# Scaled residual add on one core: the 8-row first piece of x is merged into its 64-row load, and fx is loaded first

## The chip, the core and the metric

The kernel runs on one core of a Trainium2 chip. The metric is the device time of one execution in microseconds (us); lower is better. A core has a matrix engine (PE), a vector engine (DVE), a scalar engine (ACT), a general one (POOL) and a synchronization engine (SP); each runs its own list of instructions, and they wait for one another by semaphores. Data moves between the large memory (HBM) and the on-chip memory (SBUF, 128 partitions) by 16 DMA engines. A transfer is issued by one of the instruction engines, here always SP, and is cut into descriptors, one for each contiguous run of bytes in one partition. A transfer over 128 partitions gives eight descriptors to each of the 16 DMA engines. A packet in the profile is such a descriptor, or the small write that reports a completion.

## The reference

```python
B, S, D = 512, 32, 640
x, fx: bfloat16 (B, S, D);  alpha: bfloat16 (1)

def reference(x, fx, alpha):
    return x + alpha * fx
```

Each tensor has 10,485,760 elements, 20.97 MB. Two are read and one is written: 62.92 MB. Per element there is one multiplication and one addition.

## The kernel before

Each tensor is seen as 128 partitions of 160 rows of 512 elements. One row of one partition is 1 KiB, so a partition holds 160 KiB of a tensor, and a step over rows `a` to `b` moves `b - a` KiB for each partition, in one contiguous run. The text below calls a transfer by that run: 64 rows are 64 KiB runs and 8 MiB in all, 32 rows are 32 KiB runs and 4 MiB, 8 rows are 8 KiB runs and 1 MiB.

A single buffer `buf` of 207 rows for each partition holds everything. Two tables, `F` and `X`, say where the pieces of fx and of x lie in it. The product alpha * fx is written over fx, the sum over x, and later pieces are loaded into places that earlier ones no longer need. Those reuses are what makes some loads wait for additions.

The order of the work is written out in a list, `PLAN`, which is gone through once from top to bottom. There is no loop over tiles on the chip. A line has a letter and the range of rows:

- `f`, `x`: load rows of fx or x (line 86, `nc.sync.dma_start` in `transfer`). All are issued by SP, in this order, into one queue.
- `a`: load alpha into one element (line 112), then spread it over 128 partitions with a 1 x 1 matmul against a row of ones (line 116), and copy the result to `a_f` (line 118).
- `m`: multiply rows of fx by alpha in place on DVE (line 102).
- `t`: add rows of the product to x in place on DVE (line 108).
- `s`: store rows of the sum (line 86).

The plan begins like this, with the steps that the change and the prediction speak of:

```python
PLAN = """
x 0 8
f 0 64
a
x 8 64
f 64 128
m 0 64
t 32 64
x 96 128
t 0 32
x 64 96
```

It goes on with the second multiplication (`m 64 128`), the load `f 128 160` once rows 111 to 128 are added, the load `x 128 160`, the third multiplication, and the remaining additions. The three stores `s 0 64`, `s 64 128` and `s 128 160` come last; the first of them is held back until the addition `t 64 75` is done. The first five loads wait for nothing. `x 96 128` is put where rows of the first piece of fx lay, so SP holds it until `t 32 64` has run; `x 64 96` waits likewise for `t 0 32`. Each multiplication waits for its fx and for `a_f`, and `t 32 64` waits for the product and for the x that it adds to.

SP's instructions run in order: when one waits, those behind it wait too. Once issued, a transfer's descriptors lie in the rings of the DMA engines, which take them one after another; they do not wait for the transfer before to be complete on all engines.

Of the kernel before, what the change touches and what calls it, by code (L numbers as in the profile page):

```python
# [1 line left out]

# [4 lines left out]

ACT = mybir.ActivationFunctionType
ALU = mybir.AluOpType
F32 = mybir.dt.float32  # L10
BF16 = mybir.dt.bfloat16

K = 512
P = 128


F = [(0, 64, 128), (64, 128, 64), (128, 160, 111)]
X = [(0, 64, 0), (64, 128, 143), (128, 160, 79)]
N = 160
ALL = 207  # L20

PLAN = """
x 0 8
f 0 64
a
x 8 64
f 64 128
m 0 64
t 32 64
# [3 lines that stand above are left out]
m 64 128  # L33
t 111 128
f 128 160
t 96 111
t 79 96
x 128 160
m 128 160
t 64 75  # L40
t 75 79
s 0 64
t 128 160
s 64 128
s 128 160
"""
LATE = {"s 0 64": "t 64 75"}


@with_exitstack  # L50
def kernel(
    ctx: ExitStack,
    tc: tile.TileContext,
    x: bass.AP,
    fx: bass.AP,
    alpha: bass.AP,
    out: bass.AP,
):
    nc = tc.nc

    def rows(t, a, b):

        v = t.flatten_outer_dims().rearrange("(p n) d -> p (n d)", p=P)
        assert v.shape[1] == N * K
        return v[:, a * K : b * K]

    consts = ctx.enter_context(tc.tile_pool(name="consts", bufs=1))
    psum = ctx.enter_context(tc.tile_pool(name="psum", bufs=1, space=bass.MemoryType.PSUM))
    whole = ctx.enter_context(tc.tile_pool(name="whole", bufs=1))
    ctx.enter_context(tc.manual_schedule())  # L70

    sync = mybir.DependencyInfo(mybir.DependencyClass.Sync, mybir.DependencyReason.DATA)
    buf = whole.tile([P, ALL * K], x.dtype, name="buf")
    done = []
    said = {}
    lanes = {}

    def at(pieces, a, b):

        s, _, h = next(p for p in pieces if p[0] <= a < p[1])  # L80
        e, _, g = next(p for p in pieces if p[0] < b <= p[1])
        assert h - s == g - e
        return buf[:, (a + h - s) * K : (b + h - s) * K]

    def transfer(name, out, in_):
        r = nc.sync.dma_start(out=out, in_=in_)  # L86
        if name in LATE:
            tc.add_manual_dep(r.ins, said[LATE[name]].ins.name, sync, reason="issue late")
        return r

    def load_f(a, b):
        return transfer(f"f {a} {b}", at(F, a, b), rows(fx, a, b))

    def load_x(a, b):
        return transfer(f"x {a} {b}", at(X, a, b), rows(x, a, b))

    def store(a, b):
        return transfer(f"s {a} {b}", rows(out, a, b), at(X, a, b))

    def multiply(a, b):  # L100
        term = at(F, a, b)
        return nc.vector.tensor_scalar(  # L102
            out=term, in0=term, scalar1=lanes["a_f"][:], scalar2=None, op0=ALU.mult
        )

    def total(a, b):
        s = at(X, a, b)
        return nc.vector.tensor_tensor(out=s, in0=s, in1=at(F, a, b), op=ALU.add)  # L108

    def alpha_to_lanes():  # L110
        a_1 = consts.tile([1, 1], alpha.dtype, name="a_1")
        done.append(nc.sync.dma_start(out=a_1[:], in_=alpha[None, :]))  # L112
        ones = consts.tile([1, P], alpha.dtype, name="ones")
        nc.vector.memset(ones[:], 1.0)  # L114
        a_ps = psum.tile([P, 1], F32, name="a_ps")
        done.append(nc.tensor.matmul(a_ps[:], ones[:], a_1[:], start=True, stop=True))  # L116
        lanes["a_f"] = consts.tile([P, 1], F32, name="a_f")
        return nc.vector.tensor_copy(out=lanes["a_f"][:], in_=a_ps[:])  # L118

    does = {  # L120
        "f": load_f,
        "x": load_x,
        "a": alpha_to_lanes,
        "m": multiply,
        "t": total,
        "s": store,
    }
    for step in PLAN.split("\n"):
        if step:
            what, *of = step.split()  # L130
            said[step] = does[what](*map(int, of))
            done.append(said[step])

    rest = nc.sync.nop(nofuse=True)
    for i in done[:-1]:
        tc.add_manual_dep(rest.ins, i.ins.name, sync, reason="all but the last store")


# [1 line left out]
_INS = ['x', 'fx', 'alpha']  # L140
_OUTS = [((512, 32, 640), 'bfloat16')]


# [23 lines left out]
```

## Time and profile before

| | us |
|---|---|
| median of 3 runs (150.92 to 151.01) | 151.0 |
| the profiled execution | 150.9 |
| its span, first to last instruction | 149.1 |
| DVE busy | 65.9 |
| DVE additions, 8 | 43.7 |
| DVE multiplications, 3 | 22.0 |
| DVE idle before additions, waiting for loads of x | 10.9 |
| DVE idle before multiplications, waiting for loads of fx | 7.1 |

The span is what the instruction records cover; the remaining 1.8 us of the execution lie around it. The page divides the span into 40 slices; a digit is the share of a slice, in tenths, that the DMA engines were busy, counting each packet in the slice where it starts. A timeline line gives start, duration, engine, line, operation, output and inputs, and in brackets how long the engine was idle before it and what ended that. "SPq" lines are issues of transfers: their duration is the issue, not the transfer. Where several instructions of one kind follow each other they are merged, and "x2" or "x3" counts them. Only in views of short stretches of the DMA engines can the start of the queue be seen.

### The profile page before, as it was taken

How to read it: one execution, taken by the hardware profiler on the slowest of the kernel's cores; microseconds unless marked ns; L12 is line 12 of the kernel's file. 1: busy time of each engine (PE TensorE's matmuls, PEld its weight loads, DVE VectorE, ACT ScalarE, POOL GpSimd, SP SyncE). 2: the span in 40 equal slices, each digit the busy share in tenths (PEclk: the TensorE clock that was granted, in tenths of full speed). 3: DMA queues.
4: the chain of work that ended last, by engine and by line, in shares of the span. 5: the costliest groups of instructions: out<-in, count | busy, mean ns of one | idle time of the engine just before them, and what ended most of it. 6: DMA issues, size and time to landing. Idle time of an engine off the chain costs nothing.

```text
span 149.1 us, 82 instructions
## 1 busy us (share of the span) xinstructions
PE 0.2 (0%) x1; PEld 0.1 (0%) x1; DVE 65.9 (44%) x13; POOL 0.2 (0%) x4
## 2 busy tenths in 40 slices
PE   0000000000000000000000000000000000000000
PEld 0000000000000000000000000000000000000000
DVE  0000002991079999597997907979920000000000
POOL 0000000000000000000000000000000000000000
DMA  5989695999699996999999999999796969697993
GB/s 158 615 352 563 281 563 246 492 492 492 264 545 422 422 545 299 422 422 422 422 422 422 422 431 457 457 483 527 316 563 281 563 281 563 281 563 325 466 448 167
DMA packets 1586, 62.92 MB, mean 422 GB/s; under 512 B 178, under 2 KB 178, under 8 KB 178
## 3 DMA queue, kind: packets, MB, share of 16 engines
q1 hardware_dynamic: 1586, 62.92, 98.0%
HBM read 41.94 MB, written 20.97 MB: 422 GB/s over the span
## 4 chain that ended last, share of the span: by engine, by line
DMA 51%; DVE 21%; SPq 1%; issue 0%; DVEq 0%
DMA buf<-in_x_dram 51%; DVE buf L108 21%; SPq L86 1%; SPq L112 0%; DVEq L108 0%
## 5 line engine op out<-in xcount | busy, mean ns | idle before, releaser
L108 DVE TENSOR_TENSOR buf<-buf 128x16384 bf16<-128x16384 bf16 (+4 forms) x8 | 43.7, 5487 | 10.9 <-DMA buf<-in_x_dram 10.9
L102 DVE TENSOR_SCALAR buf<-buf,a_f 128x32768 bf16<-128x32768 bf16 (+1 forms) x3 | 22.0, 7331 | 7.1 <-DMA buf<-in_fx_dram 7.1
L118 DVE COPY a_f<-a_ps 128x1 f32<-128x1 f32 x1 | 0.2, 158 | 24.2 <-PE a_ps L116 24.2
L114 DVE MEMSET ones<- 1x128 bf16 x1 | 0.2, 165 | 0.8 <-PEq L151 0.8
L116 PE MATMUL a_ps<-a,ones 1*128 1x1 bf16 x1 | 0.2, 158 | 25.0 <-DMA a<-in_alpha_dram 25.0
L151 POOL MEMSET const-bfloat16-1.0<- 128x1 bf16 x1 | 0.1, 101 | 0.0
L151 POOL MEMSET const-uint8-127<- 128x1 uint8 x1 | 0.1, 101 | 0.0
L116 PEld LDWEIGHTS <-ones 1*128 1x128 bf16 x1 | 0.1, 100 | 1.0 <-DVE ones L114 1.0
L151 POOL MEMSET const-float32-0.0<- 128x1 f32 x1 | 0.1, 98 | 0.2 <-issue 0.2
L151 POOL MEMSET const-float32-1.0<- 128x1 f32 x1 | 0.1, 98 | 0.0
## 6 DMA issues: line engine op xcount, KB each, us to landing
buf<-in_x_dram SPq DMA_DIRECT2D x3, 4096.0 KB, 20.2
buf<-in_x_dram SPq DMA_DIRECT2D x1, 7168.0 KB, 39.9
buf<-in_fx_dram SPq DMA_DIRECT2D x1, 4096.0 KB, 14.6
out_dram<-buf SPq DMA_DIRECT2D x1, 4096.0 KB, 39.4
buf<-in_x_dram SPq DMA_DIRECT2D x1, 1024.0 KB, 4.9
buf<-in_fx_dram SPq DMA_DIRECT2D x2, 41.3
out_dram<-buf SPq DMA_DIRECT2D x2, 21.4
a<-in_alpha_dram SPq DMA_DIRECT2D x1, 0.0 KB
```

Source lines behind the costliest of these rows:

```text
L86: r = nc.sync.dma_start(out=out, in_=in_)
L102: return nc.vector.tensor_scalar(out=term, in0=term, scalar1=lanes["a_f"][:], scalar2=None, op0=ALU.mult)
L108: return nc.vector.tensor_tensor(out=s, in0=s, in1=at(F, a, b), op=ALU.add)
L114: nc.vector.memset(ones[:], 1.0)
L116: done.append(nc.tensor.matmul(a_ps[:], ones[:], a_1[:], start=True, stop=True))
L118: return nc.vector.tensor_copy(out=lanes["a_f"][:], in_=a_ps[:])
L151: nc = _bacc.Bacc("TRN2", target_bir_lowering=False, num_devices=1)
```

## The change

The first line of the plan goes, and the load of x that covered rows 8 to 64 covers rows 0 to 64. The first transfer in the queue is now the load of fx, rows 0 to 64, in 64 KiB runs; alpha follows, then x, rows 0 to 64, in 64 KiB runs. Besides alpha there are ten transfers instead of eleven, of 32 and 64 KiB runs. The places in `buf`, the additions, the multiplications and the later loads and stores are as they were. The bytes moved are the same.

```diff
--- before.py
+++ after.py
@@ -20,10 +20,9 @@
 ALL = 207
 
 PLAN = """
-x 0 8
 f 0 64
 a
-x 8 64
+x 0 64
 f 64 128
 m 0 64
 t 32 64
```

## The prediction

> **What bounds the kernel now.** I read the page first, for its DMA queue and the slices.
>
> ```profile
> span 149.1 us, 82 instructions
> PE 0.2 (0%) x1; PEld 0.1 (0%) x1; DVE 65.9 (44%) x13; POOL 0.2 (0%) x4
> DMA  5989695999699996999999999999796969697993
> DMA packets 1586, 62.92 MB, mean 422 GB/s; under 512 B 178, under 2 KB 178, under 8 KB 178
> q1 hardware_dynamic: 1586, 62.92, 98.0%
> ```
>
> The one queue keeps the 16 DMA engines busy for 98.0% of the span, and VectorE (DVE) only 44%. (The digits of 6 are no gaps: a packet is counted in the slice where it starts, and a 64 KiB packet, eight of which make an engine's share of 8 MiB in some 19.4 us, lasts 2.4 us of a 3.7 us slice.) So the time is a fixed start, then 62.92 MB at the rate of the DMA engines, then a fixed end. Only three things can move it: the cost of the packets themselves, the start, or a moment when the queue runs dry.
>
> For the last of these I read the timeline.
>
> ```profile
> 0.72 0.38 SPq L86 DMA_DIRECT2D buf<-in_x_dram  x1
> 1.16 0.42 SPq L86 DMA_DIRECT2D buf<-in_fx_dram  x1
> 1.63 0.32 SPq L112 DMA_DIRECT2D a<-in_alpha_dram  x1
> 1.99 0.34 SPq L86 DMA_DIRECT2D buf<-in_x_dram  x1
> 2.37 0.57 SPq L86 DMA_DIRECT2D buf<-in_fx_dram  x1
> 25.39 8.75 DVE L102 TENSOR_SCALAR buf<-buf,a_f 128x32768 bf16<-128x32768 bf16 x1
> 42.00 17.29 DVE L108 TENSOR_TENSOR buf<-buf 128x16384 bf16<-128x16384 bf16 x2 [7.86 <-DMA buf<-in_x_dram]
> 50.72 8.93 SPq L86 DMA_DIRECT2D buf<-in_x_dram  x2
> 61.27 8.75 DVE L102 TENSOR_SCALAR buf<-buf,a_f 128x32768 bf16<-128x32768 bf16 x1 [1.99 <-DMA buf<-in_fx_dram]
> 71.06 8.76 DVE L108 TENSOR_TENSOR buf<-buf 128x8704 bf16<-128x8704 bf16 x2 [1.03 <-DMA buf<-in_x_dram]
> 80.70 4.69 DVE L108 TENSOR_TENSOR buf<-buf 128x8704 bf16<-128x8704 bf16 x1 [0.88 <-DMA buf<-in_x_dram]
> 98.00 11.26 SPq L86 DMA_DIRECT2D out_dram<-buf  x3
> 100.20 8.69 DVE L108 TENSOR_TENSOR buf<-buf 128x16384 bf16<-128x16384 bf16 x1 [1.10 <-DMA buf<-in_x_dram]
> ```
>
> The five SP issues at the top are in the queue by 2.94 us and feed it until 61 us; the next load enters at 50.7 us, 10 us before they run out. The shortest reserve is that of the first store: it enters at 98.00 us, and the load ahead of it lands at 100.1 us (0.1 us before DVE starts on it). So the queue never runs dry, and each DVE step is released by a landing.
>
> Then I read the start in the DMA view of 0 to 6 us (40 slices of 0.15 us), and two stretches of it.
>
> ```profile
> DMA  0000000000099601383999999999999999900000
> GB/s 0 0 0 0 0 0 0 0 0 0 0 273 492 109 0 55 109 273 164 437 382 382 437 382 437 437 437 382 492 382 492 765 2731 3059 874 0 0 0 0 0
> ```
>
> ```profile
> 1.73:2.03 0.30, 0.00 (x0) 0.00 (x0) 0.00 (x0) 0.00 (x0) 1.00 2.95 438
> 1.73:4.72 2.99, 0.00 (x0) 0.00 (x0) 0.00 (x0) 0.00 (x0) 1.00 1.02 340
> 3.70:4.20 0.50, 0.00 (x0) 0.00 (x0) 0.00 (x0) 0.00 (x0) 1.00 0.93 393
> ```
>
> The last two columns are the share of the 16 engines and GB/s, by the packets that start in the stretch. Nothing starts before 1.65 us, 0.93 us or more after the first issue at 0.72. In 1.73 to 2.03 us, 438 GB/s x 0.30 us / 8 KiB = 16 packets start, the first of each engine, and they last 2.95 x 0.30 x 16 / 16 = 0.885 us each. In 3.70 to 4.20 us there are 24 packets of 0.93 x 0.50 x 16 / 24 = 0.31 us. So an engine's first 8 KiB packet is 0.575 us longer than a later one. Over 1.73 to 4.72 us, 124 packets average 1.02 x 2.99 x 16 / 124 = 0.394 us, so the whole stall of the start is (0.394 - 0.31) x 124 / 16 = 0.65 us per engine: 0.575 in the first packet, some 0.07 in the others.
>
> **The change part by part.** The sum is made against the profiled execution, 150.9 us, of which 149.1 is span and 1.8 lies around it; the median of the runs is 151.0, 0.1 above it.
>
> 1. *Eight descriptors per engine go.* The piece of x of 8 rows (1 MiB, 128 descriptors of 8 KiB, eight per engine) joins the 56 rows to make 64. Price of the old pair: 8 x 0.31 = 2.48 us for the piece, and 16.94 us for the 7 MiB (fx is issued at 1.16 and lands 23.8 us later, at 24.96; the rest of x lands 39.9 us after 1.99, at 41.9). Together 19.42 us. Price of an 8 MiB load in 64 KiB rows: from 41.9 to 61.27, less 0.1 from landing to DVE's start as at 41.9, is 19.3 to 19.37 us; I take 19.36, which 7/8 of makes 16.94 and so also says that 56 KiB rows cost nothing more. The gain is 19.42 - 19.36 = 0.06 us. It lies on the path, because the queue never rests. Bounds: 0 (the rounding of 0.31 alone is 0.04) and 0.1.
>
> 2. *One transfer fewer.* Two 4 MiB loads take 71.06 - 61.27 = 9.79 and 80.70 - 71.06 = 9.64 us, 19.43 together against 19.36 for one of 8 MiB: 0.07 us, in which eight extra descriptors per engine are already counted. So the transfer itself is worth nothing beyond step 1; bounds -0.07 and 0. The Trainium skill, in DMA: Bandwidth & Descriptors, section Anatomy of one DMA — SWDGE (gpsimd) path, fits a transfer as about 2.0 us fixed plus its bytes; by that, taken for each of the queued transfers, the sum would be -2.0 us and the time 148.9. The trace does not agree for transfers queued behind one another: 0.07 us, not 2.0. The page fits another issuing path than SP's.
>
> 3. *fx goes to the front of SP's queue.* The issue at 0.72 disappears, and the fx issue moves from 1.16 to 0.72, alpha and x and the second fx by 0.44 us with it. As the queue is busy behind the first transfer, only the first issue matters. Its issue took 0.38 us for x and 0.42 for fx one place later; the extremes of the five are 0.32 and 0.57. If the first packet waits for the end of the issue, that is -0.06 to +0.19; I take 0, since place and not size seems to set it (the two fx issues, alike in size, took 0.42 and 0.57).
>
> 4. *alpha lands earlier, the whole of x no earlier.* fx would land at 24.96 - 2.48 = 22.5 us, so the matmul, the copy and the 8.75 us multiply start near 22.6 instead of 25.0 and end near 31.7. They gain nothing: DVE then waits for x until 41.9, 10.2 us instead of 7.86. That wait is also the cover. From there the plan is the same on DVE and SP; each later issue follows a landing and shifts with it, and the 2.1 us reserve at 98.00 stays.
>
> 5. *The stall of the start falls on a 64 KiB packet.* The trace shows no 64 KiB packet that starts cold. Lower end: no stall at all, -0.65 us. Upper end: the first 8 KiB's pace holds for the whole row, 8 x 0.575 = 4.6 us in place of 0.65, so +3.95. I take 0: the slow stretch in the slices ends by about 3 us, when all engines are still inside what would be their first row, and the nearest row, the second 8 KiB packets, is almost at the full pace.
>
> Sum: -0.06 + 0 + 0 + 0 + 0 = -0.06 us. The profiled execution would be 150.84, the median 150.94, so 150.9.
>
> **The rivals.**
>
> *The slow start lasts through more of the first row (slower).* All 16 engines begin within 0.3 us at the same place of their rows. With 8 KiB pieces each jumps to another row after 8 KiB; with 64 KiB rows each stays. If the slowness belongs to the row and not to the clock, each further 8 KiB at the cold pace costs 0.575 us: one gives 150.94 + 0.575 = 151.5, two 152.1, all seven 155.0. It decides the sign from 0.36 us on (0.3 for the 0.2% and 0.06 that step 1 gives), so from two thirds of one further 8 KiB. For it: the second packets are quick only after the jump, and no cold 64 KiB packet is on record. Against it: when the engines pass from the piece to 64 KiB rows of fx, still close together, the 8 MiB land in 24.96 - 5.6 = 19.36 us, the steady time.
>
> *The stall shrinks (faster).* If it comes from the turnover of small descriptors while four more issues are being put in the queue, long packets hide the 0.07 us of the later packets and perhaps part of the 0.575. With half of it: 150.94 - 0.32 = 150.6; with all, 150.3. For it: some of the later packets are also lengthened. Against it: the first packet has 0.575 of the 0.65, and a first packet remains.
>
> *A fixed cost per transfer (faster).* If each transfer costs the fixed 2.4 us that the first shows beyond its data (landing 4.9 us after its issue, 2.48 of it data), 148.6. Against it stands step 2.
>
> *The queue runs dry before the first store (slower).* It would need a step between the landing of x and 98.00 to come over 1 us later than now against the landings (2.1 us of reserve less the 0.93 from issue to first packet). The DVE steps there are unchanged.
>
> **How the numbers follow.** About 0.2% (0.3 us) is what a measurement of this kernel can tell from no change. My forecast, the stall unchanged and so no measurable difference, has a chance of 0.43, with its own range of 150.7 to 151.3 (steps 1 to 3). The slow start that lasts: 0.35, most of it at one or two further 8 KiB, 151.4 to 152.2; a third of it beyond. The shrinking stall: 0.18, 150.3 to 150.7. The fixed cost: 0.02. The dry queue: 0.02. So faster 0.20, same 0.43, slower 0.37. The range of 150.3 to 152.3 leaves out a third of 0.35, the fixed cost and part of the dry queue, some 0.16.
>
> **What would show it.** Step 1: 1,442 packets (128 rows and 16 completions fewer), and 8 MiB loads that land 19.36 us apart. Step 3: first packets again near 1.75 us. Step 4: the multiply at 22.9 us and the first add at 41.9 to 42.0. Step 5: a share over GB/s for the first 16 packets that gives 2.4 + 0.6 = 3.0 us each; 3.6 us or more is the slow rival, 2.5 the fast one. If the first add starts within 0.1 us of 41.94 and the time still moves, my reading of the rest is wrong and the queue must show a gap.

## The result, and the profile after

| | before | after |
|---|---|---|
| median of 20 runs, us | 150.97 | 151.19 |
| lowest to highest, us | 150.87 to 151.04 | 151.09 to 151.37 |
| profiled execution, us | 150.9 | 151.17 |
| its span, us | 149.1 | 149.4 |

The ratio is 1.0017, with a 95% interval of 1.0011 to 1.0023: the change costs 0.22 us. The forecast was a gain of 0.06 us, too small to tell. The ratio lies within the 0.2% that the forecast called no difference, but its interval excludes a ratio of 1, and the sign is the opposite one. In a later repeat on another chip the ratio was 1.0037 (1.0024 to 1.0049).

These are lines of the timeline of the changed kernel, with start, duration, engine, line, operation, and in brackets the idle time before it; others are left out. Every line from the first addition on stands about 0.25 us later than before.

```profile
0.73 0.38 SPq L85 DMA_DIRECT2D buf<-in_fx_dram  x1
1.16 0.31 SPq L111 DMA_DIRECT2D a<-in_alpha_dram  x1
1.52 0.34 SPq L85 DMA_DIRECT2D buf<-in_x_dram  x1
1.91 0.61 SPq L85 DMA_DIRECT2D buf<-in_fx_dram  x1
22.58 0.16 PE L115 MATMUL a_ps<-a,ones 1*128 1x1 bf16 x1 [22.58 <-DMA a<-in_alpha_dram]
22.96 8.75 DVE L101 TENSOR_SCALAR buf<-buf,a_f 128x32768 bf16<-128x32768 bf16 x1
42.24 17.30 DVE L107 TENSOR_TENSOR buf<-buf 128x16384 bf16<-128x16384 bf16 x2 [10.53 <-DMA buf<-in_x_dram]
61.52 8.75 DVE L101 TENSOR_SCALAR buf<-buf,a_f 128x32768 bf16<-128x32768 bf16 x1 [1.98 <-DMA buf<-in_fx_dram]
98.25 11.24 SPq L85 DMA_DIRECT2D out_dram<-buf  x3
100.44 8.69 DVE L107 TENSOR_TENSOR buf<-buf 128x16384 bf16<-128x16384 bf16 x1 [1.08 <-DMA buf<-in_x_dram]
```

The first addition is at 42.24 instead of 42.00, so all that is lost is lost before it. From there to the last addition pass 58.20 us, as before (100.20 - 42.00). The page has the packets that the change should leave, and a queue as full as before:

```profile
DMA packets 1442, 62.92 MB, mean 421 GB/s; under 512 B 162, under 2 KB 162, under 8 KB 162
q1 hardware_dynamic: 1442, 62.92, 97.9%
```

The loss is at the start. This stretch of the changed kernel contains the start of the first packet of each DMA engine, and no other; the last two columns are the share of 16 engines and GB/s.

```profile
1.70:2.30 0.60, 0.00 (x0) 0.00 (x0) 0.00 (x0) 0.00 (x0) 1.00 5.42 1748
```

1748 GB/s x 0.60 us / 64 KiB is 16 packets, and 5.42 x 0.60 = 3.25 us is the mean length of one. A later 64 KiB packet takes 2.42 us (19.36 / 8), so the stall is 0.83 us per engine, against 0.65 us for the eight 8 KiB packets of the kernel before.

The engines are also further apart. In the DMA view of 4.4 to 6.0 us (40 slices of 0.04 us), each start of a 64 KiB packet adds 1638 GB/s to its slice. First the kernel before, where these are the first packets of fx behind the 8 KiB piece, then the changed kernel, where they are the second packets of fx:

```profile
GB/s 410 205 205 1024 0 614 205 614 1843 205 3277 3482 1843 3277 4916 1638 3277 0 0 1638 1638 0 0 0 0 0 0 0 0 0 0 0 0 0 0 0 0 0 0 0
```

```profile
GB/s 0 0 0 0 0 0 0 0 1638 1638 0 3277 3277 1638 0 0 3277 0 0 0 3277 3277 0 0 0 0 3277 0 0 1638 0 0 0 0 0 0 0 0 0 0
```

Both begin in the ninth slice, at 4.72 us. The last engine follows at 5.20 to 5.24 us before and at 5.56 to 5.60 us after: a spread of 0.5 and of 0.85 us. A transfer has landed when its slowest engine is done, so the step that waits for it sees the last engine and not the mean.

The lag is still there when x lands. In the DMA view of 40.8 to 42.0 us (40 slices of 0.03 us), a start of a 64 KiB packet adds 2185 GB/s; these are the first packets of the load behind x, so each start follows the end of one engine's share of x. The kernel before, then the changed kernel:

```profile
GB/s 0 0 0 0 0 0 2185 0 0 4369 4369 2185 2185 2185 6554 2185 2185 2185 0 0 2185 0 2185 0 0 0 0 0 0 0 0 0 0 0 0 0 0 0 0 0
```

```profile
GB/s 0 0 0 0 0 2185 0 2185 0 2185 2185 0 4369 2185 0 2185 0 2185 0 0 0 0 4369 2185 2185 0 0 0 0 2185 2185 0 0 2185 0 0 0 0 0 0
```

The packet records of the traces give the times themselves, from the small write with which each engine reports its share done. The mean engine ends its share of x at 41.20 us before and 41.34 after, 0.14 later; the slowest ends at 41.46 and 41.80, 0.34 later. The landing itself comes 0.44 us after the slowest engine's end before and 0.35 after, at 41.90 and 42.15. So the 0.25 us are 0.14 of the mean engine and 0.20 of a wider lag of the slowest, less 0.09 that this one pair of profiles shows between the last end and the landing.

### The profile page after: what moved, and what is told of

It is laid out like the page before. It is cut to its first block, busy times and chain, and to the rows that moved or that the text cites. A ratio compares the mean times of both kernels' runs of the same rounds, so it can differ in the third digit from the quotient of the medians.

```text
span 149.4 us, 80 instructions
## 1 busy us (share of the span) xinstructions
PE 0.2 (0%) x1; PEld 0.1 (0%) x1; DVE 65.9 (44%) x13; POOL 0.2 (0%) x4
## 2 busy tenths in 40 slices
DMA packets 1442, 62.92 MB, mean 421 GB/s; under 512 B 162, under 2 KB 162, under 8 KB 162
## 3 DMA queue, kind: packets, MB, share of 16 engines
q1 hardware_dynamic: 1442, 62.92, 97.9%
## 4 chain that ended last, share of the span: by engine, by line
DMA 51%; DVE 21%; SPq 0%; issue 0%; DVEq 0%
DMA buf<-in_x_dram 51%; DVE buf L107 21%; SPq L85 0%; SPq L111 0%; DVEq L107 0%
## 5 line engine op out<-in xcount | busy, mean ns | idle before, releaser
L115 PE MATMUL a_ps<-a,ones 1*128 1x1 bf16 x1 | 0.2, 158 | 22.6 <-DMA a<-in_alpha_dram 22.6
## 6 DMA issues: line engine op xcount, KB each, us to landing
buf<-in_fx_dram SPq DMA_DIRECT2D x2, 40.8
```

## The experiments

Each diff is against the kernel before; a kernel that starts from the changed one shows the change too. All ratios are to runs of the kernel before on the same chip. Where a diff adds a function, the line that ties it to its letter in the plan is left out. Durations of first packets are worked out from stretches like the one above: share x length of the stretch x 16 / number of packets. The experiments ran on four chips, and the changed kernel itself was run beside them on one of these only, where it lost 0.37% and not 0.17%; so ratios from different sections compare to no better than 0.2%. Each start was profiled in one execution.

### Which tensor, and how long a piece

First the other tensor at the front, with the 64 KiB runs kept:

```diff
-x 0 8
+x 0 64
 f 0 64
 a
-x 8 64
 f 64 128
```

> The first transfer is x in 64 KiB runs, then fx, then alpha; ten transfers besides alpha, as in the changed kernel, but the tensor that starts the queue is that of the kernel before. Row theory (the stall of the start grows with the time an engine stays in its first row): as the changed kernel, 151.2 us, first packets of about 3.25 us. Tensor theory (the first touch of fx is dearer than that of x): 150.9 us, first packets of about 3.0 us. Queue theory (the issues behind the first transfer, which come 0.44 us earlier in the changed kernel, disturb the first packets): about 151.0 us, since the large issues stand as in the kernel before.

155.04 us, ratio 1.0277 (1.0257 to 1.0296): no theory had that. I had overlooked that fx now lands second. The first multiplication runs at 42.34 us where the first addition used to stand, so the additions, and the loads that wait for their places, come 9 us later, and the queue runs short (its share falls to 96.3%). But the start can be read apart from the rest:

```profile
1.70:2.60 0.90, 0.00 (x0) 0.00 (x0) 0.00 (x0) 0.00 (x0) 1.00 3.62 1165
```

3.62 x 0.90 = 3.26 us for each of the 16 first packets, as with fx at the front. The tensor theory predicted 3.0.

Then fx at the front, with the short piece back:

```diff
-x 0 8
-f 0 64
+f 0 8
+f 8 64
 a
-x 8 64
+x 0 64
```

> The 8 KiB piece comes back, but as 8 rows of fx (fx 0 to 8, fx 8 to 64, alpha, x 0 to 64). Row theory: as the kernel before, 150.97 us, first packets of about 0.9 us. Tensor theory: 151.2 us. Queue theory: 150.97 us, as there are again eleven transfers and the same issues in the first 3 us.

150.93 us, ratio 1.0000 (0.9991 to 1.0009), first packets of 1.26 x 0.65 = 0.82 us:

```profile
1.70:2.35 0.65, 0.00 (x0) 0.00 (x0) 0.00 (x0) 0.00 (x0) 1.00 1.26 202
```

The short piece alone brings back the time, whichever tensor it is cut from, and though fx, alpha and x are in the order of the changed kernel. That leaves the length of the first packets, or the number of transfers.

Four runs change the length alone, with x at the front as before:

```diff
-x 0 8
+x 0 32
 f 0 64
 a
-x 8 64
+x 32 64
```

> The first piece of x is 32 rows instead of 8 (x 0 to 32, fx 0 to 64, alpha, x 32 to 64). Row theory: near the changed kernel, 151.1 to 151.2 us, first packets of about 2.0 us against 1.21 for a later one. Tensor theory and queue theory: as the kernel before, 150.95 us.

> The kernel before with a first piece of 16 rows (x 0 to 16, fx 0 to 64, alpha, x 16 to 64). Row and length theories: between the 8-row and the 32-row piece, 150.97 to 151.1 us relative to 150.95 before, first packets of 1.3 to 1.4 us against 0.61 for a later one. A theory by which only very short pieces differ: as the 32-row piece, 151.13.

> The kernel before with a first piece of 4 rows. By the same thought (the 64 KiB packets would begin near 3.3 us): between the 2-row piece and the 8-row piece, about 151.05 us relative to 150.95 before. If the stall is over once an engine has left its first run, whatever the time: 150.95 us or less.

> The first piece of x is 2 rows (2 KiB runs, 256 KiB in all). Row theory: the engines leave their first rows after 2 KiB and the stall shrinks, 150.7 to 150.9 us. Clock theory (the start costs each engine a fixed time, whatever the packet) and tensor and queue theories: 150.95 us as the kernel before, and a fixed stall would fall on several packets of an engine.

| first piece of x | first packet, us | the same later, us | ratio (interval) |
|---|---|---|---|
| 2 rows | | | 1.0012 (1.0004 to 1.0021) |
| 4 rows | | | 1.0005 (0.9997 to 1.0014) |
| 8 rows (before) | 0.885 | 0.31 | 1 |
| 16 rows | 1.18 | 0.61 | 0.9997 (0.9989 to 1.0006) |
| 32 rows | 2.03 | 1.21 | 1.0011 (1.0002 to 1.0020) |
| 64 rows (changed kernel, fx) | 3.25 | 2.42 | 1.0017 (1.0011 to 1.0023) |

The kernels with 2 and 32 rows ran on one chip, those with 4 and 16 on another; the last row is the result above.

The stretches of the kernel with 16 rows and of that with 32 rows:

```profile
1.70:2.60 0.90, 0.00 (x0) 0.00 (x0) 0.00 (x0) 0.00 (x0) 1.00 1.31 291
```

```profile
1.70:2.30 0.60, 0.00 (x0) 0.00 (x0) 0.00 (x0) 0.00 (x0) 1.00 3.39 874
```

1.31 x 0.90 = 1.18 us (1.3 to 1.4 was expected), 0.57 us over a later one; 3.39 x 0.60 = 2.03 us, 0.82 over. So the stall of the first packet does not grow in step with its length: 0.575, 0.57, 0.82 and 0.83 us for 8, 16, 32 and 64 KiB. In these profiles it takes one step, between 16 and 32 KiB, and the time seems to take it too, though the intervals of 16 and 32 rows touch. The first packet of 8 KiB alone is not a steady figure: in three other profiles of kernels that begin with an 8-row piece its stall was 0.26 to 0.51 us. The stall of the whole start is the better measure: 0.47 to 0.65 us in the four profiles with 8 rows, about 0.6 with 16, and 0.72 to 0.84 in the five profiles that begin with 64 KiB packets on all 16 engines. The kernel with 32 rows has the eleven transfers of the kernel before and loses all the same, so the number of transfers is not the reason. Shorter than 8 rows is no better: 2 rows, which the row theory had faster, are slower beyond the interval, and 4 rows are not to be told from no change. The packet records show where the shorter pieces lose. With 2 rows the mean engine ends its share of x at 41.29 us, against 41.23 with the 8-row piece of fx on the same chip, but the slowest at 41.75 against 41.50, and the profiled executions took 151.15 and 150.92 us. With 4 rows against 16, also on one chip, the mean engine ends at 41.24 and 41.27, the slowest at 41.71 and 41.49, and the executions took 151.27 and 151.02 us. These kernels lose by the lag of the slowest engine, and hardly by the mean one.

One more run keeps the short packets going longer than a single 2-row piece does:

```diff
-x 0 8
+x 0 2
+x 2 4
+x 4 6
+x 6 8
 f 0 64
```

> The 8-row piece of x as four pieces of 2 rows, one after the other. If what matters is that the first 2.5 to 3 us are filled with short packets, and the single 2-row piece lost because the 64 KiB packets began at 2.7 us, while the engines were still in the stretch of the stall: as the kernel before, 150.95 to 151.05 us (32 packets of 2 KiB cost about 0.2 us more than 8 of 8 KiB). If 2 KiB packets are worse in themselves: 151.15 us or more.

152.59 us, ratio 1.0097 (1.0082 to 1.0113), far over both expectations. I had counted 0.2 us for 32 packets of 2 KiB in place of 8 of 8 KiB. The fx issue comes only at 2.58 us, behind four others, and a stretch of 1.70 to 5.10 us has a share of 0.88 at 261 GB/s, so the DMA engines are poorly filled there and move little. Nothing follows from it for the question; it shows that short packets for longer are not a cure.

### The issues behind the first transfer

In the changed kernel three more issues follow within 1.8 us of the first, and I suspected that putting their descriptors into the queues held up the first packets. Here x, and the second fx behind it, are held back by a memset of part of x's place, which the load must wait for:

```diff
-x 0 8
 f 0 64
+z 0 16
 a
-x 8 64
+x 0 64
...
+    def hold(a, b):
+        return nc.vector.memset(buf[:, a * K : b * K], 0.0)
```

> The changed kernel, but a memset of the first 16 rows of x's place runs first on DVE (an estimate of 4 to 5 us from the additions' rate), and the issue of x 0 to 64, with the second fx behind it, waits for it; the queue has 19 us of fx to go, so the wait itself costs nothing. Queue theory (descriptors of later transfers being put in the rings while the first packets run are what stalls them): the first 16 packets fall from 3.25 us to 2.6 us or so, first add near 41.7 us, 150.6 to 150.9 us. Row theory and address theory (the engines' reads collide in HBM): first packets stay at 3.25 us, 151.2 us.

The memset lasted 3.47 us and x was issued at 5.15 us, after 12 of the 16 first packets had ended. They still took 5.25 x 0.60 = 3.15 us, and the ratio was 1.0039 (1.0027 to 1.0052). The same in the kernel before, with `z 8 24` ahead of alpha:

> The same hold in the kernel before: the issue of x 8 to 64, with alpha ahead of it as before and the second fx behind it, waits for a memset of 16 rows of x's place; x 0 to 8 and fx 0 to 64 are issued as before. Queue theory: the first 16 packets fall below 0.88 us and the time by 0.1 to 0.4 us, 150.6 to 150.85. Row and address theories: 0.88 us and 150.95 us.

150.79 us, ratio 0.9999 (0.9990 to 1.0007). The first packets were shorter, as the queue theory had it: 0.57 us by the packet records. But the same kernel without the hold had 0.68 us on another chip (below), the whole start was stalled by 0.50 us against 0.47 there, and the time did not move. So the queue theory falls for the change: without the two large issues beside them, 64 KiB first packets stay long, and 8 KiB ones gain no time that shows. A gain of up to 0.15 us lies within the interval.

### A cold start, and the place in HBM

Are the first packets long because nothing has run before? Here a 2-row piece runs first, then fx waits until the engines stand idle:

```diff
-x 0 8
+x 0 2
+z 128 144
 f 0 64
 a
-x 8 64
+x 2 64
```

> A first transfer of 2 rows of x (256 KiB), then fx 0 to 64 only after a memset of 16 rows of its place (4 to 5 us), so that the engines have been used, stand still, and begin fx's 64 KiB runs together. The time is worse by some 3 us of idle queue and is not the point. Cold theory (the first use of the engines or of the path is what costs): the first 64 KiB packets last about 2.45 us. Row, address and queue theories: about 3.25 us again.

The 64 KiB packets of fx began at 6.1 us, on engines that had been used, with this stretch:

```profile
6.10:6.80 0.70, 0.00 (x0) 0.00 (x0) 0.00 (x0) 0.00 (x0) 1.00 4.55 1498
```

4.55 x 0.70 = 3.19 us each. The stall is not that of a first use alone; it came back after an idle time of about 3 us. (155.28 us in one execution, as the idle queue costs.)

The other way was to move the runs in HBM, so that partitions are 64 KiB apart and not 160, in the changed kernel:

```diff
-        v = t.flatten_outer_dims().rearrange("(p n) d -> p (n d)", p=P)
-        assert v.shape[1] == N * K
-        return v[:, a * K : b * K]
+        s, e = next(p for p in ((0, 64), (64, 128), (128, 160)) if p[0] <= a < p[1])
+        v = t.rearrange("b s d -> (b s d)")[s * P * K : e * P * K]
+        v = v.rearrange("(p n) -> p n", p=P)
+        return v[:, (a - s) * K : (b - s) * K]
```

> The changed kernel, with each piece of 64, 64 and 32 rows taken from one contiguous stretch of each tensor, so that runs of neighbouring partitions lie 64 KiB apart in HBM instead of 160 KiB (32 KiB for the last piece); the arithmetic pairs the same elements of x and fx. Address theory: the stall of the first packets (0.83 us now) changes clearly, in either direction, and the time with it, by 0.2 us or more. Cold and queue theories: 3.25 us first packets and 151.2 us, no change.

151.09 us, ratio 1.0019 (1.0010 to 1.0027), first packets of 5.29 x 0.60 = 3.17 us. The length of the first packets does not hang on the distance of the runs, for these two distances. This speaks against reads that collide because of their addresses, though other distances were not tried. For the time it is less clear. The changed kernel was not run on this chip, where the held one above lost 0.39%, and by the packet records the slowest engine was 0.36 us behind the mean one at the end of x here and 0.62 in the held kernel. Whether the distance changes the lag is not shown.

### Length of the packet, or time spent in one run

A long first packet also keeps the engine in one run of HBM for longer. Here the whole first piece of fx comes in 8 KiB packets, but a partition's run still gives four of them one after the other; that an engine takes these four in a row is the idea of the run, and the profile does not show it:

```diff
-x 0 8
-f 0 64
+h 0 64 0
+h 0 64 1
 a
-x 8 64
+x 0 64
...
+    def load_f_half(a, b, i):
+        def half(v):
+            return v.rearrange("p (c two n) -> p c two n", two=2, n=8 * K)[:, :, i, :]
+
+        return transfer(f"h {a} {b} {i}", half(at(F, a, b)), half(rows(fx, a, b)))
```

> The changed kernel, but fx 0 to 64 comes in two transfers of 8 KiB descriptors, first the even and then the odd 8 KiB of each 64 KiB run, so that an engine has short descriptors and still works through one partition's run before it goes to the next. Cost of the short descriptors alone: 64 of 0.31 us in place of 8 of 2.42 us, some 0.4 us. Row theory (the stall goes with staying in one run): the stall of the changed kernel stays, 151.5 to 151.6 us. Length theory (the stall goes with the length of the descriptor itself, short ones let the engines even out): the start of the kernel before, first packets of 0.8 to 0.9 us and later ones of 0.31, 151.3 us.

151.67 us, ratio 1.0048 (1.0036 to 1.0060): above both and nearer to that of the row theory, but on a chip where the changed kernel was not run, so the time does not decide. The start can be read, in a stretch of it and in a later one of the same kind of packets:

```profile
1.70:6.00 4.30, 0.00 (x0) 0.00 (x0) 0.00 (x0) 0.00 (x0) 1.00 0.98 347
7.00:12.00 5.00, 0.00 (x0) 0.00 (x0) 0.00 (x0) 0.00 (x0) 1.00 1.01 428
```

In the first, 347 x 4.30 / 8.192 = 182 packets last 0.98 x 4.30 x 16 / 182 = 0.370 us; in the second a packet lasts 0.309. The stall is (0.370 - 0.309) x 182 / 16 = 0.69 us per engine, near the 0.65 of the kernel before and not the 0.83 of the changed one. So it seems to go with the length of the packet and not with the time in one run, by this one profile. The packet records account for the time: against the 16-row piece of x on the same chip the mean engine ends its share of x 0.48 us later, of which 0.43 is the price of the short packets, 64 x 0.309 against 8 x 2.418, and the slowest 0.62 later; the profiled execution is 0.61 us longer.

### Once more, on another chip

The changed kernel and the kernel before again, and a 16-row piece cut from fx (`f 0 16`, `f 16 64`, alpha, `x 0 64`), all on one chip:

> The changed kernel once more. If its start stall is a property of the kernel: first packets of 3.2 to 3.3 us, the slowest engine some 0.4 us behind the mean, 0.1 to 0.25% over the kernel before. If the profiled execution was a draw among many: first packets anywhere between 2.9 and 3.3 us.

> The kernel before once more: ratio 1.000 within 0.1%; first packets of 0.85 to 0.9 us and a start stall of about 0.65 us if that is a property of the kernel, below 0.55 or above 0.75 if it is a draw.

> fx 0 to 16 first, then fx 16 to 64, alpha, x 0 to 64. If the length of the first packets decides and the tensor does not: as the 16-row piece of x, ratio 0.999 to 1.0005, first packets of about 1.18 us. If fx at the front is worse in itself: 1.001 or more.

The changed kernel: 151.37 us, ratio 1.0037 (1.0024 to 1.0049). The kernel before: 1.0004 (0.9994 to 1.0013). The 16-row piece of fx: 1.0004 (0.9995 to 1.0013), with first packets of 1.90 x 0.60 = 1.14 us, no faster than 8 rows. The stretches of the changed kernel, and then of the kernel before, where 1.70 to 4.60 us holds nearly all 8 KiB packets:

```profile
1.70:2.30 0.60, 0.00 (x0) 0.00 (x0) 0.00 (x0) 0.00 (x0) 1.00 5.23 1748
```

```profile
1.70:4.60 2.90, 0.00 (x0) 0.00 (x0) 0.00 (x0) 0.00 (x0) 1.00 0.99 350
```

The first gives 3.14 us, a stall of 0.72. The second gives 350 x 2.90 / 8.192 = 124 packets of 0.99 x 2.90 x 16 / 124 = 0.37 us, a stall of (0.37 - 0.31) x 124 / 16 = 0.47. Each is smaller than in the first profiles. The first packets of the kernel before took 0.68 us, not 0.85 to 0.9, and its stall lies below 0.55, which I had called the sign of a draw; the changed kernel's 3.14 us and 0.37% lie outside their bands too. So the size of a stall is not a fixed property of the kernel, and one profile on one chip gives it to no better than 0.2 us. The difference between the two kernels kept its sign: 0.25 us here, 0.18 there. The starts of the following 64 KiB packets spread over 1.05 us in the changed kernel and 0.45 in the kernel before. By the packet records the mean engine ends its share of x 0.21 us later in the changed kernel and the slowest 0.54, and the profiled execution is 0.58 us longer. These are the changed kernel's starts:

```profile
GB/s 0 0 0 0 0 1638 0 1638 1638 3277 0 3277 1638 1638 0 1638 0 1638 3277 0 0 0 1638 0 0 1638 0 0 0 0 0 1638 0 0 0 0 0 0 0 0
```

### All engines together, or each for itself

The last question was whether an engine stalls because 15 others begin with it. A few partitions of fx are loaded alone first; the whole load waits for them and loads them again.

```diff
-x 0 8
+p 0 64 4
 f 0 64
 a
-x 8 64
+x 0 64
...
+    def load_f_some(a, b, p):
+        return transfer(f"p {a} {b} {p}", at(F, a, b)[0:p], rows(fx, a, b)[0:p])
```

> The changed kernel with 4 partitions of fx 0 to 64 loaded first, alone, by as many engines as there are partitions, and then all 128 (the first load's bytes again), which waits for the first to land. Contention theory (the stall comes from 16 engines beginning together): the four lone 64 KiB packets take 2.5 to 2.75 us, the 16 that follow about 3.2 us. Latency theory (filling the path is what costs): the lone ones take 3.0 us or more as well. The time is worse by the 4 us of the extra load and says nothing.

```profile
1.60:1.80 0.20, 0.00 (x0) 0.00 (x0) 0.00 (x0) 0.00 (x0) 1.00 10.37 1311
```

1311 x 0.20 / 65.5 = 4 packets, of 10.37 x 0.20 x 16 / 4 = 8.3 us each: neither theory. Four engines together moved 256 KiB at the pace of about one. So the run did not answer, and the next two used partitions four apart (`[0 : 4 * p : 4]` in both places):

> As the run with four lone partitions, but partitions 0, 4, 8 and 12 in place of 0 to 3 for the first load. If neighbouring partitions share one way into the on-chip memory, the four packets no longer take 8 us. Then, contention theory (the stall comes from 16 engines beginning together): 2.45 to 2.75 us. Latency theory: 3.0 us or more, as when 16 begin. The 16 packets that follow: about 3.2 us.

> Eight lone engines, partitions 0 to 28 in steps of four. Contention theory: between four engines and sixteen, 2.6 to 3.0 us. Latency theory: the same as with four engines.

With four engines, the lone packets and then the 16 that follow:

```profile
2.20:2.40 0.20, 0.00 (x0) 0.00 (x0) 0.00 (x0) 0.00 (x0) 1.00 3.77 1311
6.70:7.60 0.90, 0.00 (x0) 0.00 (x0) 0.00 (x0) 0.00 (x0) 1.00 3.45 1165
```

With eight:

```profile
2.20:2.80 0.60, 0.00 (x0) 0.00 (x0) 0.00 (x0) 0.00 (x0) 1.00 2.47 874
6.80:7.60 0.80, 0.00 (x0) 0.00 (x0) 0.00 (x0) 0.00 (x0) 1.00 3.92 1311
```

Four lone packets take 3.77 x 0.20 x 16 / 4 = 3.02 us, eight take 2.47 x 0.60 x 16 / 8 = 2.96, and the 16 behind them 3.45 x 0.90 = 3.11 and 3.92 x 0.80 = 3.14 us. Most of the stall, 0.55 to 0.6 us, came with four and eight engines as well, so it does not need 16 that begin together; company adds 0.1 to 0.2 us. That is the latency theory, with a small share for contention, by one execution each; a single engine alone was not tried.

## Why the prediction was wrong

**Step 1, eight descriptors fewer.** Held: 1,442 packets, and what the rows after the start show leaves no other price for it. Fx lands 22.1 us after 0.73 and x 40.63 us after 1.52, at 42.15: 19.3 us apart, as taken. The reading of 19.36 us left out the 0.1 us that the sentence itself takes off (61.27 - 41.9 - 0.1 is 19.27), but the packet records of the kernel before bear it out: from the end of x to the end of the next 8 MiB the mean engine takes 19.35 us. The gain of 0.06 us was not measured by itself, and it is small beside what follows.

**Step 2, one transfer fewer.** Nothing, as taken: the 32-row kernel has eleven transfers and loses, and fx with an 8-row piece has eleven and equals the kernel before. The rival of a fixed cost per transfer, at 148.6, is out by 2.6 us.

**Step 3, fx at the front.** Held: its issue took 0.38 us, as that of x had at the same place, so place and not size set it. That the tensor is of no account is shown by the kernel with an 8-row piece of fx, whose ratio is 1.0000.

**Step 4, alpha earlier, x no earlier.** The matmul started at 22.58 (22.6 was said), the multiplication at 22.96 (22.9), though fx landed at 22.8 and not at 22.5, and the wait for x grew to 10.53 us (10.2 was said), as the extra 0.25 us of the landing lies in it. The reserves at the stores moved with the landings, and the dry queue did not come.

**Step 5, the stall, is the one that failed.** "I take 0" for a 64 KiB packet that starts cold was mis-sized. The first packets took 3.25 us and not 3.0, below the 3.6 that was to mark the slow rival, so the stall rose from 0.65 to 0.83 us, by 0.18; on the other chip from 0.47 to 0.72. I had taken the quick second 8 KiB packets as the sign that the stall ends by the clock whatever the packet. By the runs it depends on the packet: with first packets of 8 or 16 KiB it is shorter than with 32 or 64. With the 0.06 of step 1 this makes +0.12 us for the mean engine, and the packet records show 0.14. The landing moved by 0.25. The rest is the lag of the slowest engine behind the mean one, which grew from 0.26 to 0.46 us, less the 0.09 between its end and the landing. That second term was missing from the sum altogether: I priced the mean engine, and the landing waits for the last.

**The rivals.** The slow start that lasts had the right place and sign, but its mechanism and price were not right. It priced each further 8 KiB at the cold pace at 0.575 us; there was 0.18 in all, and next to none between 32 and 64 KiB. Its reason, staying in one row, is not borne out by the run with short packets in one run, and what it saw in all engines beginning together is 0.1 to 0.2 us of it. The shrinking stall did not come: holding the later issues back gained no time that shows.

**What stays open.** Why a first packet of 32 KiB or more waits 0.2 us longer than one of 16 KiB or less, and why the engines then end further apart, no run shows. The same holds for the lag behind a 2-row or 4-row piece. The size of the loss differed between two runs of the changed kernel, on different chips (1.0017 and 1.0037), and each start was profiled in one execution for each kernel and chip.

## What to carry to other kernels

When a queue is full from start to end and the price of its packets stays the same, what is left to win or lose lies at its two ends: read the first microseconds of the DMA view with the packets counted one by one. A first packet of 8 or 16 KiB per engine made the kernel some 0.2 to 0.6 us faster here than one of 32 or 64 KiB; between 8 and 16 KiB nothing could be told apart, and no other layout tried here beat the kernel before. Price the slowest engine and not the mean one, since a landing waits for it. In a queue that never rests its lag lasts: in the changed kernel the engines were still 0.82 us apart at 90 us and 0.61 at the end.

## What the runs showed of the hardware

- DMA engines that start from idle on a 64 KiB packet took 3.0 to 3.3 us for it in the mean of each run, against 2.42 in a running queue. They did so after an idle stretch as at the first use (3.19 us), and with four engines as with sixteen (3.02 against 3.11 us).
- The 16 engines of a full queue kept the distances of their start: the ends of one transfer were spread over 0.84 us at 22 us and over 0.82 at 90 us in the changed kernel, 0.48 and 0.48 in the kernel before.
- Four transfers of 64 KiB into four neighbouring partitions, by four engines, took 8.3 us each; into partitions four apart 3.02 us. The Trainium skill, in SBUF — State Buffer, section Door 1: The DMA port swizzle, puts partitions 0 to 3 on one port of the memory, and each of 0, 4, 8 and 12 on a port of its own. The trace agrees: 256 KiB in 8.3 us is 32 GB/s, near the 64 KiB in 2.42 us, 27 GB/s, of one engine in a running queue. That the shared port is what slowed the four engines is an inference from the two runs.
